# An attention and MoE kernel on one core: a gate one chunk later, down-scores in other PSUM banks, and a copy shared by two engines

## The chip, the core and the metric

The kernel runs on one core of one Trainium2 chip. A core has five engines with instruction streams of their own: TensorE (PE, matrix products into PSUM; PEld is its weight load), VectorE (DVE), ScalarE (ACT), GpSimd (POOL) and SyncE (SP, which here only issues transfers). Each works through its own list in order and waits at semaphores for the others. Transfers between the device's memory and on-chip SBUF run on 16 DMA engines that all queues share; SP's go through queue q1, POOL's through queue q0, and instructions are fetched through small queues of their own (q8, q14). The metric is the device time of one execution in microseconds (us). PSUM is the accumulator memory; the program uses three tiles of two banks (PA[0] to PA[2]) and two of one bank (PM[0], PM[1]).

## The reference

Two parts, one after the other:

```python
# q, k, v: (8 batches, 8 heads, 576 positions, 64)
q_d, k_d, v_d = mean over 4 neighbouring positions          # 144 positions
out_d     = softmax(q_d k_d^T / 8) v_d, each row repeated 4 times
out_local = softmax(q k^T / 8 where |i - j| < 4) v
x = (out_d + out_local) as (4608 tokens, 512)
h = x @ w_in                                                # 512 x 2048
y = (h * sigmoid(1.702 h)) @ w_out                          # 2048 x 512
```

Inputs and output are float32; the kernel multiplies in bf16.

## The kernel before, in words

**Tiling.** The 4608 tokens are nine groups of 512. For a group g, `mm1` makes h transposed in 16 blocks of 128 hidden columns (`hps_mm`, L616: four products of 128x512 each, one for each of the four chunks of 128 model columns), ACT applies SiLU into `gT`, and `mm2` makes four output tiles of 128 tokens with 16 products each (L672). A batch has 576 tokens, so the attention of batch g + 1 is woven into the products of group g: a dictionary of steps says ahead of which product a step of the attention is written. For group 0 the places are `POS_0 = [16, 18, 27, 54, 68, 60, 76]` and `VDP_0 = 52`, counted over 16 blocks of `mm1` and then the products of `mm2`; so 52 is ahead of the 37th product of `mm2`. The order of `mm2` in group 0 takes w_out in four parts of four hidden blocks, the third being wanted at its 33rd product.

**Attention of one batch.** Heads go in pairs (hp 0 to 3), pairs in two halves (qd 0 for pairs 0 and 1, qd 1 for pairs 2 and 3).
- q and k are loaded by POOL's queue (`load_qk`), transposed by DVE (`prep_1`, L260) and pooled over four positions by POOL (`pool_qk`, two additions for each of k and q). `pool_qk(b, qd, names)` can do k alone or q alone.
- `scores` makes the banded local scores (L351), `scores_d` the pooled ones (L369); ACT takes their exponentials (`exp_local`, `exp_down`) into es and eds.
- v is loaded by SP in ten transfers (`load_v`, L214), two for each of five chunks of positions, and cast to bf16 chunk by chunk (`prep_v`). For batches 0 and 1 the pooled v is made by products with a selection matrix (`prep_vd_pe`, L312) that ACT copies to vd (L321).
- `av_local` (L408) and `av_down` (L430) multiply with v; the row sums come along as a 65th column. `normalise` on DVE divides (L441, L443) into y.
- For batch 0, `turned` brings y to the transposed layout by products (`transp_sum`, L483, L493, L507) and `copy_x` writes xT (L520, L524): four copies for a pair, two for each of the two interleaved sets of positions (`par`).

**Order.** The schedule is manual: every engine carries out its instructions in the order in which the program writes them. Around the change, batch 0 is written out by hand ahead of the loop over groups. POOL pools the first half, then writes one element into w_in's buffer from v's buffer. That copy is the gate: it can't run before a certain v transfer has landed, and the load of w_in's first part (512 of 2048 columns) can't be issued before the gate. After it come the pooling of the second half, w_in's other two parts, the q and k loads of batch 1, two of four parts of w_out, and a memset.

On TensorE, `warm(n)` issues n products of zeros that write PM[0] and PM[1] in turn from one call to the next; the call ahead of `turned` writes PM[0]. Then batch 0's first products with h are placed between the four `turned` by `part`, which takes hidden blocks and model chunks: blocks 0 and 1 accumulate in the PM banks, 2 to 5 in halves of PA[1] and PA[2].

After that, the loop begins. On DVE it starts with the four transposes for batch 1 and then the gate of batch 1's v load, one element copied from w_out's first part:

```python
            load_v(1, gate=after(w_out_bf[0:1, 0, 0:1], nc.vector))
            pool_qk(1, 1)
            nc.gpsimd.tensor_copy(
                out=w_out_bf[0:1, 8, 0:1], in_=vf[1][0:1, 3, 0, 0:1]
            )
            load_w_out(2)
            load_w_out(3)
```

The last lines are one more gate of that kind: w_out's third and fourth part wait for v 1's fourth chunk.

Of the kernel before, what the change touches and what calls it, by code (L numbers as in the profile page):

```python
# [10 lines left out]
AF = mybir.ActivationFunctionType  # L11
# [8 lines left out]
def kernel(  # L20
# [9 lines left out]
    nc = tc.nc  # L30
    B, H, S, D = q.shape
    SD = S // 4
    HP = H // 2
# [5 lines left out]
    inv_sqrt_d = 1.0 / math.sqrt(D)  # L39
# [18 lines left out]
    w_in_bf = persist.tile([128, n_dmc, d_ff], BF16, name="w_in_bf")  # L58
# [5 lines left out]
    eds = [persist.tile([128, 2, 464], BF16, name=f"ed{i}") for i in range(2)]  # L64
# [3 lines left out]
    PA = [psum.tile([128, 2, 512], FP32, name=f"pa{i}") for i in range(3)]  # L68
    PM = [psum.tile([128, 512], FP32, name=f"pm{i}") for i in range(2)]
    turn = {"a": 0, "m": 0}  # L70

    def ps_tile(n=None):
        if n is None:
            n = turn["a"] % 3
            turn["a"] += 1
        return PA[n]

    def pm_tile():
        turn["m"] += 1
        return PM[turn["m"] % 2]  # L80
# [107 lines left out]
    qf, kf, vf = {}, {}, {}  # L188
# [46 lines left out]
    def load_w_in(c, n):  # L235
        nc.gpsimd.dma_start(
            out=w_in_bf[:, :, c : c + n],
            in_=bass.AP(
                tensor=moe_w_in.tensor, offset=moe_w_in.offset + c,
                ap=[[d_ff, 128], [128 * d_ff, n_dmc], [1, n]],  # L240
            ),
        )
# [23 lines left out]
    def prep_qk(b, qd):  # L266
        prep_1("k", b, qd)
        prep_1("q", b, qd)

    def pool_qk(b, qd, names="kq"):  # L270
        for name, src in (("k", kT), ("q", qT)):
            if name not in names:
                continue
            sv = src[b, qd].rearrange("p (j f) a -> p j f a", f=4)
            t1 = work.tile([128, SD, 2, 2], FP32, name="pq", tag="pq")
            nc.gpsimd.tensor_tensor(  # L276
                out=t1, in0=sv[:, :, 0:2, :], in1=sv[:, :, 2:4, :], op=ALU.add
            )
            if name == "k":
                dst = kdT[qd][:, 0:SD, :]  # L280
            else:
                t = work.tile([128, SD, 2], BF16, name=f"qdT{qd}", tag=f"qdT{qd}", bufs=1)
                qdT[b, qd] = t
                dst = t
            nc.gpsimd.tensor_tensor(
                out=dst, in0=t1[:, :, 0, :], in1=t1[:, :, 1, :], op=ALU.add
            )
# [73 lines left out]

    def scores_d(b, qd, sd=None):
        sd = sd or ps_tile()
        for kc in range(3):
            for a in range(2):
                for r in range(4):
                    rows = slice(32 * r, 32 * r + 32)
                    j = r % 2
                    nc.tensor.matmul(  # L369
                        sd[64 * j : 64 * j + 64, r // 2, SD * kc : SD * kc + SD],  # L370
                        lhsT=kdT[qd][rows, 48 * kc : 48 * kc + 64, a],
                        rhs=qdT[b, qd][rows, :, a],
                        start=(a == 0), stop=(a == 1),
                        tile_position=(32 * r, 64 * j),
                    )
        return sd
# [8 lines left out]
    def exp_down(qd, sd):  # L385
        nc.scalar.activation(  # L386
            out=eds[qd][:, :, 0:432], in_=sd[:, :, 0:432],
            func=AF.Exp, scale=inv_sqrt_d / 16.0,
        )
# [6 lines left out]
    def av(b, hp, n=None):  # L396
        o = ps_tile(n)
        av_local(b, hp, o)
        av_down(b, hp, o)
        return o  # L400

    def av_local(b, hp, o):
        E, vb = es[hp], vbs[b % 2]
        for i in range(5):
            for par in range(2):
                for j in range(2):
                    pos = j if par == 0 else 1 - j
                    nc.tensor.matmul(  # L408
                        o[64 * pos : 64 * pos + 64, par, 65 * i : 65 * i + 65],
                        lhsT=E[64 * par : 64 * par + 64, j, 60 * i : 60 * i + 64],  # L410
                        rhs=vb[64 * par : 64 * par + 64, i, 2 * hp + j, :],
                        start=True, stop=True,
                        tile_position=(64 * par, 64 * pos),
                    )

    def av_down(b, hp, o):
        Ed, vd, u = eds[hp // 2], vds[b % 2], hp % 2

        blocks = [(kc, x, 0) for kc in range(3) for x in range(2)]
        blocks += [(0, 0, 1), (0, 1, 1), (1, 0, 1), (2, 0, 1)]  # L420
        if True:
            for kc, x, c2 in blocks:
                for j in range(2):
                    pos = j if x == 0 else 1 - j
                    c0 = 65 * (5 + c2)
                    q0 = SD * kc + 48 * (min(x + c2, 1) + x)
                    last = x == c2 == 1
                    if last:
                        q0 = 0
                    nc.tensor.matmul(  # L430
                        o[64 * pos : 64 * pos + 64, j, c0 : c0 + 65],
                        lhsT=Ed[64 * j : 64 * j + 48, u, q0 : q0 + 64],
                        rhs=vd[64 * j : 64 * j + 48, kc, hp, :],
                        start=(kc == 0), stop=(kc == 2 or last),
                        tile_position=(64 * j, 64 * pos),
                    )

    def normalise(o):
        ov = o[:, :, 0:455].rearrange("p x (c e) -> p x c e", e=65)
        rc = work.tile([128, 2, 7, 1], FP32, name="rc", tag="rc")  # L440
        nc.vector.reciprocal(rc, ov[:, :, :, 64:65])  # L441
        y = work.tile([128, 2, 7, D], BF16, name="y", tag="y", bufs=4)
        nc.vector.tensor_tensor(  # L443
            out=y, in0=ov[:, :, :, 0:D],
            in1=rc.to_broadcast([128, 2, 7, D]), op=ALU.mult,
        )
        return y
# [69 lines left out]
    def copy_x(b, hp, x):  # L517
        t0 = b * S
        for par in range(2):
            nc.scalar.copy(  # L520
                out=sub(xT[hp], t0 + 3 + 57 * par, (114, 5), (1, 57)),
                in_=sub(x[par], 3 - 3 * par, (57, 5), (1, 57)),
            )
            nc.scalar.copy(  # L524
                out=sub(xT[hp], t0 + 573 * par, (1, 3)),
                in_=sub(x[par], 285 * par, (1, 3)),
            )
# [10 lines left out]
    def sub(t, off, *dims):  # L538
        return bass.AP(
            tensor=t.tensor, offset=t.offset + off,  # L540
            ap=[list(t.ap[0])] + [list(d) for d in dims],
        )
# [25 lines left out]
    def warm(n):  # L568
        if n:
            t = pm_tile()  # L570
            for _ in range(n):
                nc.tensor.matmul(
                    t, lhsT=wz[:, 0:128], rhs=wz, start=True, stop=True
                )

    def attention(b, slots=None):
        st = {}

        def s_pe(qd):
            st["s", qd] = scores(b, qd)  # L580
            st["d", qd] = scores_d(b, qd)
# [41 lines left out]
    def new_gT():  # L623
        return moe_sb.tile([128, n_ffc, TG], BF16, name="gT", tag="gT")
# [80 lines left out]
    o, y, x = {}, {}, {}  # L705
# [19 lines left out]
    sp = scores(0, 0, barred=True)  # L725
    exp_local(0, sp)
    prep_qk(0, 1)
    nc.gpsimd.tensor_copy(out=w_in_bf[0:1, 0, 0:1], in_=vf[0][0:1, 1, 0, 0:1])
    load_w_in(0, 512)
    pool_qk(0, 1)  # L730
    load_w_in(512, 512)
    load_w_in(1024, 1024)
    for qd in range(NQ):
# [6 lines left out]
    make_up()  # L740
    warm(5)
    sd = scores_d(0, 0)
    prep_v(0, nc.scalar, i=slice(0, 1))
    exp_down(0, sd)
# [5 lines left out]
        prep_v(0, nc.vector, i=slice(i, i + 1))  # L750
    warm(6)
    prep_vd_pe(0, PA[2])
    o[0] = PA[0]
    av_local(0, 0, o[0])
    av_down(0, 0, o[0])
    y[0] = normalise(o[0])
    sd = scores_d(0, 1, PA[1])
    exp_down(1, sd)
    nc.scalar.preload_act_table_set("silu_and_others")
    for hp in range(1, 3):  # L760
        o[hp] = PA[hp]
        av_local(0, hp, o[hp])
        av_down(0, hp, o[hp])
        y[hp] = normalise(o[hp])
    warm(1)

    gT0 = new_gT()
    acc = PM + [PA[n][:, u, :] for n in (1, 2, 0) for u in range(2)]
# [7 lines left out]
    def turned(hp, n):  # L776
        x = PM if n is None else [PA[n][:, u, :] for u in range(2)]
        transp_sum(y[hp], x)
        copy_x(0, hp, x)
# [20 lines left out]
    for g in range(n_groups):  # L800
        b = g + 1
        if g == 0:
# [6 lines left out]
                out=w_out_bf[0:1, 8, 0:1], in_=vf[1][0:1, 3, 0, 0:1]  # L809
# [61 lines left out]
```

The softmax here doesn't subtract the row's maximum and nothing guards it: scores larger than these inputs give would overflow.

## Time and profile before

| what | value |
|---|---|
| median of 8 executions | 333.97 us (332.78 to 336.96) |
| the profiled execution | 334.05 us |
| its span, first to last instruction | 332.3 us |
| TensorE busy | 316.2 us, 95% of the span |
| DVE, ACT, POOL busy | 130.9, 184.6, 138.4 us |
| dense products of `mm1` (L616), 544 in the group | 121.6 us busy |
| dense products of `mm2` (L672), 528 in the group | 121.7 us busy |
| moved by DMA | 41.36 MB, mean 124 GB/s |
| v load (L214) | 80 transfers of 128 KB, 5.4 us from issue to landing (median) |
| w_in | two parts of 512 KB, 6.3 us; one of 1024 KB, 9.8 us |

The profile is of one execution. Its own time (334.05 us) is the one that the span belongs to; what is over, 1.75 us, lies around the first and last instruction. A line of a timeline gives start, length, engine, line of the program, operation, output and inputs, how many instructions were merged, and in brackets the engine's idle time just before and what ended it. In the chain of waits, each line is a piece of the chain that ended last: start, length, what it was. TensorE's granted clock is given as a share of full speed (one digit for each fortieth of the span, in tenths).

### The profile page before, as it was taken

The page shows a single profiled execution, that of the slowest core. Times are in us where ns is not written, and L with a number is a line of the kernel's source. Part 1 is how long each engine was busy: PE and PEld are TensorE (multiplying, and loading weights), DVE is VectorE, ACT ScalarE, POOL GpSimd, SP SyncE. Part 2 cuts the span into 40 slices and gives each one's busy share as a digit, 9 for nine tenths or more (in the row PEclk, how much of TensorE's full clock was granted, in tenths as well). Part 3 has the DMA queues.
Part 4 walks back from the last instruction along what each step waited for, and adds up shares of the span by engine and source line. Part 5 has one row for each costly group of instructions (what it writes and reads, how often), then busy time and mean ns, then how long its engine had stood idle before and what let it go on. Part 6 is the DMA issues. An engine that isn't in the chain of part 4 may idle for free.

```text
span 332.3 us, 11272 instructions
## 1 busy us (share of the span) xinstructions
PE 316.2 (95%) x5043; PEld 159.4 (48%) x5043; DVE 130.9 (39%) x213; ACT 184.6 (56%) x323; POOL 138.4 (42%) x168
## 2 busy tenths in 40 slices
PE   8737999999999999999999999999999999999995
PEld 3425445444554445444544454455445554444444
DVE  4846402482167307730773077406740570000000
ACT  2524488257755665576656665666476746425611
POOL 7791834019900991099109910991089000000000
PEclk9967899999999999999999999999999999999999
DMA  7999969998931994199419940994180110011011
GB/s 123 172 184 211 176 136 190 194 184 212 189 94 54 215 190 119 46 210 194 128 40 215 208 114 36 198 212 109 59 175 3 36 65 32 2 64 63 2 59 67
DMA packets 63552, 41.36 MB, mean 124 GB/s; under 512 B 44048, under 2 KB 54416, under 8 KB 63504
## 3 DMA queue, kind: packets, MB, share of 16 engines
q1 hardware_dynamic: 55056, 26.95, 35.3%
q0 software_dynamic: 8304, 13.63, 23.4%
q8 instruction: 39, 0.64, 0.8%
q14 instruction: 9, 0.07, 0.1%
q10 hardware_dynamic: 144, 0.07, 0.1%
HBM read 44.83 MB, written 9.44 MB: 163 GB/s over the span
## 4 chain that ended last, share of the span: by engine, by line
PE 89%; SPq 4%; DVE 2%; DMA 2%; issue 1%; ACT 1%; DVEq 0%; ACTq 0%
PE pm L616 36%; PE pm L672 35%; SPq L214 4%; PE pa L351 3%; PE pa L616 2%; DMA vf<-in_v_dram 2%; PE pa L408 2%; PE pa L369 2%; PE pa L430 2%; PE pa L457 2%; PE pa L672 1%; PE pm L687 1%; DVE y L443 1%; PE pa L483 1%; ACT vd L321 0%
## 5 line engine op out<-in xcount | busy, mean ns | idle before, releaser
L616 PE MATMUL pm<-xT,w_in_bf 128*128 128x512 bf16 x544 | 121.6, 380 | 0.5 <-DVE xT L559 0.5
L672 PE MATMUL pm<-w_out_bf,gT 128*128 128x512 bf16 x528 | 121.7, 380 | 0.0
L627 ACT ACTIVATE gT<-pm 128x512 bf16<-128x512 f32 x136 | 81.1, 598 | 44.5 <-PE pm L616 44.5
L616 PEld LDWEIGHTS <-w_in_bf 128*128 128x128 bf16 x576 | 55.8, 98 | 67.9 <-issue 2.0
L672 PEld LDWEIGHTS <-gT 128*128 128x128 bf16 x560 | 51.8, 98 | 59.5 <-issue 0.2
L276 POOL TENSOR_TENSOR pq<-kT 128x576 f32<-128x576 bf16 x16 | 18.5, 1157 | 105.2 <-DVE kT L260 105.2
L394 DVE TENSOR_TENSOR es<-es,mask 128x600 bf16<-128x600 bf16 x28 | 20.1, 731 | 96.7 <-ACT es L380 95.9
L657 ACT ACTIVATE osb<-pm 128x512 f32<-128x512 f32 (+2 forms) x35 | 20.8, 593 | 39.3 <-PE pm L672 34.9
L532 ACT COPY od<-pa 128x384 f32<-128x384 f32 (+1 forms) x56 | 18.4, 412 | 30.8 <-DVE y L443 22.4
L443 DVE TENSOR_TENSOR y<-pa,rc 128x896 bf16<-128x896 f32 x32 | 34.9, 1092 | 1.1
L553 DVE TENSOR_TENSOR xT<-pa,od 128x570 bf16<-128x570 f32 x28 | 21.1, 754 | 10.4 <-ACT od L532 10.3
L380 ACT ACTIVATE es<-pa 128x600 bf16<-128x600 f32 x32 | 19.8, 669 | 6.6 <-PE pa L351 6.3
L297 POOL TENSOR_TENSOR v<-v 112x512 f32<-112x512 f32 x18 | 22.8, 1266 | 0.0
L659 DVE TENSOR_SCALAR osb<-pm 128x128 f32<-128x128 f32 x1 | 0.3, 292 | 55.3 <-ACT osb L657 55.3
L260 DVE STREAM_TRANSPOSE kT<-kb 128x576 f32<-128x576 f32 x16 | 20.0, 1250 | 3.1 <-DMA kb<-in_k_dram 3.0
L260 DVE STREAM_TRANSPOSE qT<-qb 128x576 f32<-128x576 f32 x16 | 19.9, 1241 | 0.9 <-DMA qb<-in_q_dram 0.8
L276 POOL TENSOR_TENSOR pq<-qT 128x576 f32<-128x576 bf16 x16 | 18.5, 1157 | 0.0
L291 POOL CAST vb<-vf 128x2560 bf16<-128x2560 f32 (+1 forms) x11 | 17.0, 1570 | 0.0
L441 DVE RECIPROCAL rc<-pa 128x14 f32<-128x14 f32 x32 | 7.7, 241 | 22.9 <-PE pa L430 22.9
L351 PEld LDWEIGHTS <-kT 32*64 32x64 bf16 x1280 | 11.9, 104 | 6.9 <-issue 5.9
L351 PE MATMUL pa<-qT,kT 32*64 32x60 bf16 x1280 | 13.8, 203 | 1.5 <-issue 1.1
L386 ACT ACTIVATE ed<-pa 128x864 bf16<-128x864 f32 x16 | 14.3, 896 | 1.5 <-PE pa L369 1.5
(86 smaller groups left out, 252.1 us busy)
## 6 DMA issues: line engine op xcount, KB each, us to landing
vf<-in_v_dram SPq DMA_DIRECT2D x80, 128.0 KB, 5.4
out_dram<-osb SPq DMA_DIRECT2D x35, 256.0 KB, 2.0
v<-in_v_dram SPq DMA_DIRECT2D x36, 192.0 KB, 5.2
kb<-in_k_dram POOLq DMA_DIRECT2D x16, 288.0 KB, 6.8
qb<-in_q_dram POOLq DMA_DIRECT2D x16, 288.0 KB, 7.7
w_out_bf<-in_moe_w_out_dram POOLq DMA_DIRECT2D x4, 512.0 KB, 12.7
w_in_bf<-in_moe_w_in_dram POOLq DMA_DIRECT2D x2, 512.0 KB, 6.3
w_in_bf<-in_moe_w_in_dram POOLq DMA_DIRECT2D x1, 1024.0 KB, 9.8
```

What stands on the lines that cost most here:

```text
L260: nc.vector.transpose(out=t32.rearrange("p (i c) -> p c i", c=18), in_=store[b, qd].bitcast(FP32).rearrange("p (c d) -> p c d", c=18),)
L276: nc.gpsimd.tensor_tensor(out=t1, in0=sv[:, :, 0:2, :], in1=sv[:, :, 2:4, :], op=ALU.add)
L297: eng.tensor_tensor(out=t1[0:112], in0=x[:, :, 0:2, :], in1=x[:, :, 2:4, :], op=ALU.add)
L351: nc.tensor.matmul(sp[r // 2][64 * par : 64 * par + 64, r % 2, 60 * i : 60 * i + 60], lhsT=kT[b, qd][rows, k0 : k0 + 64, a], rhs=qT[b, qd] ...
L380: nc.scalar.activation(out=es[2 * qd + u][:, :, 0:300], in_=sp[u][:, :, 0:300], func=AF.Exp, scale=inv_sqrt_d,)
L394: nc.vector.tensor_tensor(out=ev, in0=ev, in1=mask, op=ALU.mult)
L443: nc.vector.tensor_tensor(out=y, in0=ov[:, :, :, 0:D], in1=rc.to_broadcast([128, 2, 7, D]), op=ALU.mult,)
L553: eng.tensor_tensor(out=sub(xT[hp], t0 + 3, (57, 2), (114, 5), (1, 57)), in0=sub(x, 3, (509, 2), (57, 5), (1, 57)), in1=sub(od, 3, (57, 2) ...
L616: nc.tensor.matmul(acc, lhsT=w_in_bf[:, dmc, ffc * 128 : (ffc + 1) * 128], rhs=xT[dmc][:, g * TG : g * TG + TG], start=(dmc == 0), stop=(d ...
L627: nc.scalar.activation(out=gT[:, ffc, :], in_=acc, func=AF.Silu, scale=GELU_SCALE)
L657: eng.activation(out=osb, in_=ap, func=AF.Copy, scale=1.0 / GELU_SCALE)
L672: nc.tensor.matmul(ops[t], lhsT=gT[:, ffc, t * 128 : (t + 1) * 128], rhs=w_out_bf[:, ffc, :], start=(ffc == 0), stop=(ffc == n_ffc - 1),)
```

## The change

Three edits, all in the preparation of batch 0:

1. POOL pools k of the second half ahead of the gate of w_in, and q behind w_in's first load. The gate reads v 0's third chunk (index 2) instead of its second, so w_in's first load waits for the fifth v transfer where it waited for the third.
2. Batch 0's second down-scores go to PM[0] and PM[1], one bank for each pair of the half, instead of to PA[1]; their exponential is two ACT instructions of 432 columns instead of one of 864. TensorE's order is now: `av_local` of pairs 0 and 1, `av_down` of pairs 0 and 1, the down-scores, one warm product, then both products of pair 2. Before, it was pair 0, the down-scores, pair 1, pair 2, the warm product.
3. In `copy_x`, the two copies of the second set of positions (`par` 1) of the last pair are made by DVE instead of ACT.

```diff
     def scores_d(b, qd, sd=None):
         sd = sd or ps_tile()
+        bank = sd if sd is PM else [sd[:, u, :] for u in range(2)]
...
                     nc.tensor.matmul(
-                        sd[64 * j : 64 * j + 64, r // 2, SD * kc : SD * kc + SD],
+                        bank[r // 2][64 * j : 64 * j + 64, SD * kc : SD * kc + SD],
...
     def copy_x(b, hp, x):
         t0 = b * S
         for par in range(2):
-            nc.scalar.copy(
+            cp = nc.vector.tensor_copy if par and hp == HP - 1 else nc.scalar.copy
+            cp(
                 out=sub(xT[hp], t0 + 3 + 57 * par, (114, 5), (1, 57)),
                 in_=sub(x[par], 3 - 3 * par, (57, 5), (1, 57)),
             )
-            nc.scalar.copy(
+            cp(
                 out=sub(xT[hp], t0 + 573 * par, (1, 3)),
                 in_=sub(x[par], 285 * par, (1, 3)),
             )
...
     prep_qk(0, 1)
-    nc.gpsimd.tensor_copy(out=w_in_bf[0:1, 0, 0:1], in_=vf[0][0:1, 1, 0, 0:1])
+    pool_qk(0, 1, "k")
+    nc.gpsimd.tensor_copy(out=w_in_bf[0:1, 0, 0:1], in_=vf[0][0:1, 2, 0, 0:1])
     load_w_in(0, 512)
-    pool_qk(0, 1)
+    pool_qk(0, 1, "q")
     load_w_in(512, 512)
     load_w_in(1024, 1024)
...
     prep_vd_pe(0, PA[2])
-    o[0] = PA[0]
-    av_local(0, 0, o[0])
-    av_down(0, 0, o[0])
-    y[0] = normalise(o[0])
-    sd = scores_d(0, 1, PA[1])
-    exp_down(1, sd)
-    nc.scalar.preload_act_table_set("silu_and_others")
-    for hp in range(1, 3):
+    for hp in range(2):
         o[hp] = PA[hp]
         av_local(0, hp, o[hp])
+    for hp in range(2):
         av_down(0, hp, o[hp])
         y[hp] = normalise(o[hp])
+    scores_d(0, 1, PM)
+    for u in range(2):
+        nc.scalar.activation(
+            out=eds[1][:, u, 0:432], in_=PM[u][:, 0:432],
+            func=AF.Exp, scale=inv_sqrt_d / 16.0,
+        )
+    nc.scalar.preload_act_table_set("silu_and_others")
     warm(1)
+    o[2] = av(0, 2, 2)
+    y[2] = normalise(o[2])
```

## The prediction

> **What bounds the kernel now.** I read the page first (shares, clock row, chain), then the chain of waits in order of time, then the merged timeline from 0 to 74 us, and last the DMA records. The page says where nothing is to be had:
>
> ```profile
> PE 316.2 (95%) x5043; PEld 159.4 (48%) x5043; DVE 130.9 (39%) x213; ACT 184.6 (56%) x323; POOL 138.4 (42%) x168
> PEclk9967899999999999999999999999999999999999
> PE 89%; SPq 4%; DVE 2%; DMA 2%; issue 1%; ACT 1%; DVEq 0%; ACTq 0%
> ```
>
> TensorE is 95% busy, and the two dense lines (L616, L672) carry 70% of the chain. Only the first 40 us are bound by something else: slices 3 to 5 are where the clock is not full. All three edits lie there, so the question is how much sooner TensorE enters the dense stream, and whether that head start survives. The chain of waits, from the last v loads on (start, length, what):
>
> ```profile
> 13.25 0.64 SPq L214
> 13.94 7.31 DMA vf<-in_v_dram
> 22.29 0.81 ACT vd L321
> 23.14 0.54 PE pa L430 x19
> 23.68 0.89 PE pa L369 x19
> 24.60 0.90 ACT ed L386
> 30.20 1.49 issue
> ```
>
> Read it as a story. The tenth v transfer is issued at 13.94 and lands 7.31 us later, though the eight before it have landed by 15.5. Everything after hangs on it: the cast, the selection matmuls (L312), ACT's copy into vd, av_down, the second down-scores, their exp (TensorE stands still for 0.90 us, since the scores sit in PA[1], which av_local needs next), then a stall of 1.49 us that waits for nothing in the program. The timeline names the other clients:
>
> ```profile
> 13.04 0.80 POOL L236 DMA_DIRECT2D w_in_bf<-in_moe_w_in_dram  x1 [0.30 <-POOL w_in_bf L728]
> 13.86 1.16 POOL L276 TENSOR_TENSOR pq<-kT 128x576 f32<-128x576 bf16 x1
> 17.27 1.22 DVE L291 CAST vb<-vf 128x512 bf16<-128x512 f32 x2
> 21.35 0.43 DVE L291 CAST vb<-vf 128x512 bf16<-128x512 f32 x1 [2.85 <-DMA vf<-in_v_dram]
> 27.43 0.55 PE L483 MATMUL pm<-up,y 128*64 128x285 bf16 x4
> 31.61 1.26 DVE L260 STREAM_TRANSPOSE kT<-kb 128x576 f32<-128x576 f32 x1 [0.80 <-DMA kb<-in_k_dram]
> 37.98 0.14 DVE L708 CAST vf<-w_out_bf 1x1 f32<-1x1 bf16 x1 [1.22 <-DMA w_out_bf<-in_moe_w_out_dram]
> 46.81 0.18 POOL L808 CAST w_out_bf<-vf 1x1 bf16<-1x1 f32 x1 [6.34 <-DMA vf<-in_v_dram]
> 58.67 1.03 PE L672 MATMUL pm<-w_out_bf,gT 128*128 128x512 bf16 x4
> ```
>
> From the DMA records, per half us: where v runs alone (12 to 13 us) 377 and 378 of its 256 B records pass; from 16.0 to 18.5, beside w_in's first part, only 347 in five halves, with 387 records of 1024 B for w_in. From 18.5, w_in being through, 322 in one half. So w_in takes the last chunk's place, and DVE idles 2.85 us for it.
>
> **The change, part by part.**
>
> *1. w_in later.* POOL ends the batch-0 pooling at 11.10 and idles 1.46 us at the old gate. Now the k pooling of the second pair goes there (1.15 + 0.67, so 11.10 to 13.0). The new gate waits for the fifth v transfer, whose landing record is at 13.74: cast at 13.8, issue at 14.28 (the old spacing of 0.48), 1.24 us later than 13.04. The old issue needed 2.0 us to its first dozens of records and 2.5 to full pace (62 in the half from 15.5), so the new one gets up to pace about 16.8. The last two v transfers are issued at 13.25 and 13.94 as now; 2.3 us later they can flow (the first of their records come after 15.5), together 1024 records at 750 per us: the ninth is through at 16.3, most of the tenth by 16.8, its rest at the contended 140 per us by about 18. It cannot land later than now (21.25), nor does it help before DVE is free: vb's second and third chunk end at 18.49. So the fourth cast runs from 18.5 to 18.93 at best, against 21.78 now: between 0 and 2.85 us. I take 2.7, near the good end, because 370 of 512 records precede w_in. POOL may overlap less with DVE's selector work (2.03 us for two small operations beside POOL's pooling); if these shorten, up to 0.8 more.
>
> Behind the waiting POOL gate stand the q pooling (15.10 to 17.4 instead of 15.89 to 18.21), the two other w_in parts, the four qk loads of batch 1, two w_out parts and the memset. The k pooling has left that line, so all these issue about 0.8 us sooner, at 17.4 instead of 18.15. w_in's first part is wanted at 31.94 now (28.9 then) and landed at 20.29; its last landed at 28.78, first needed after 40. SP's queue is passed by nothing.
>
> *2. Down-scores to the MoE banks, two av_local ahead.* Now av_down to the first L483 takes 27.43 - 23.14 = 4.29 us. Then: av_local of pair 1 (0.49) goes under ACT's vd copy (0.80), which now covers only pair 0's 0.49, with 0.3 idle. Left: two av_down (0.54 each), scores (0.94), the exp of the first bank, the warm matmul (0.54), av of pair 2 (0.49 + 0.54, or 0.71 if it interleaves as the two pairs did, 1.42 for both). The stall is not gone: warm(1) writes PM[0], the very bank that the first exp reads, so it waits. That exp has 432 columns; from 0.598 for 512 and 0.896 for 864, 0.53, as an estimate. Sum 3.7 to 4.25 with 0.1 of gaps; I take 4.0, so 0.3 gained (0.05 to 0.6). The two exps cost ACT 1.06 instead of 0.89; with the table load (1.28) they end at 24.6, before the first copy_x at 25.6. y of pairs 0 and 1 (1.09 each) is done while TensorE makes scores.
>
> The next thing is the 1.49 us stall. Two stalls of TensorE's queue (1.08 ending at 14.35, 1.49 ending at 31.69) end 1.3 to 1.6 us after a 16 KB packet of the instruction queue (ended at 12.8 and 30.4). The block seems asked for some 5.7 us ahead, by the sequencer passing an instruction that the old program reaches right after the wait for exp at 25.54 and the new one after its wait at 22.8. So I move the stall along with the rest, gain 3.0, cost 0.
>
> By the Trainium skill (Runtime: NRT & Kernel Launch, Instruction fetch mechanics), crossing a 16 KiB boundary is mostly hidden; the 1.49 us here contradict that, and with no stall the sum would be 4.5 instead of 3.0.
>
> *3. Half of the last x copy on DVE.* ACT's four copies end at 37.96 and their reader (L616 with the last d_model chunk) starts at 39.18, behind ten matmuls of 0.216: ending 0.4 sooner gives 0. The price is the order on DVE: the copies (0.4 + 0.15, from half of the 0.754 of a 570-column sum) stand ahead of four transposes and the gate of v 1, which now run from 31.61, before TensorE has ended the transposition (37.08, then about 34.1). Transposes: 34.65 to 39.8 instead of 31.61 to 36.77. Scores of batch 1 (49.20, then 46.2) and POOL's pooling for them (39.8) leave 6 us: hidden. The v 1 gate moves from 37.98 to 39.8, and with it SP's ten v loads (38.26 to 40.1), their seventh landing (46.75 to 48.6), POOL's gate L808, w_out's third part (issue 49.1, landing 53.34 to 55.2) and v's casts. TensorE wants that part at 58.67 - 3.0 = 55.7. Slack falls from 5.3 to 0.5 us, so it stays hidden, barely; if that cover is gone it costs us for us. Casts end at 53.5, wanted at 56.6. This is what is late next.
>
> *Clock.* Granted is half from 19.4 to 29.6 and again from 33.05 to 36.46, in steps of 3.41. The step from 22.8 to 26.2 was 64% busy and did not lift; that from 29.6 to 33.05, 56% busy with the 1.49 stall in it, dropped. The same stall 3 us earlier falls into the step before and drops the next in the same way, so six dense matmuls run at 0.43 again: 0.
>
> The Trainium skill (TensorE: Matmul & The Clock Gate, Part 1) lets the clock fall only after an idle window of about 3.4 us; by that the new stall would cost no half-speed step and the sum would be 4.3 (six times 0.215 more). The 56% step speaks against it.
>
> Sum: 2.7 + 0.3 + 0 + 0 = 3.0. From 72 us on TensorE is dense at a period of 33.40 us per group (106.04, 139.44), so nothing gives it back. The profiled execution is 334.05 (span 332.3 and 1.75 around it), 0.08 above the median of the eight; 334.05 - 3.0 = 331.0.
>
> **The rivals.**
> *Chunk still late.* w_in reaches full pace before the tenth transfer flows, as now. For it: 140 records per us beside w_in mean 3.7 us for 512. Then it lands about 20.2 and 1.0 is gained, with part 2 1.3 at most: 332.7. Against: the 1.24 us. This is also "does not do what it says".
> *More is gained.* The instruction block comes in time, or the clock is up from 22.8 (that step's forerunner would be over 80% busy): 1.0 to 1.5 more, 329.6. Against: w_out's slack of 0.5 caps what is gained only ahead of the transposition on DVE's path.
> *Slower: w_out's third part becomes the bound.* Place: the 33rd matmul of L672. It decides against the change once that part lands 3 us after 55.7, that is v 1 coming 3.5 us slower than now. Nearest row: v 2, loaded beside q and k, took 12.1 us to its first landing against 2.9 for v 1; with 9.2 more the stall is 8.7 and the time 339.8. Against: w_out's second part ends about 39.9, so v 1 runs alone.
>
> **How the numbers follow.** About 0.5% (1.7 us) is what a measurement of this kernel can tell from no change. Forecast 0.58 (330.2 to 332.2), more gained 0.14, chunk late 0.18 (332.3 to 334), slower 0.10. So faster 0.72, same 0.18, slower 0.10. The range leaves out the slower case and the tips of the two others: 329.0 to 333.9.
>
> **What would show it.** In the new profile: w_in's first issue near 14.3; the fourth vb cast at 18.5 to 19 with almost no idle ahead; av_local of both pairs during the vd copy; a wait of warm on ACT of about 0.5; the first L483 near 24.4; an issue stall near 27 to 28.6; transposes from about 34.6; no wait at L672's 33rd matmul near 55.7; the first group's dense stream 3 us ahead and the same distance at the end. Wrong if the cast waits past 20, or if TensorE idles before w_out's third part.

## The result, and the profile after

The changed kernel takes 331.75 us (median of 19 executions, 327.41 to 333.43) against 333.98 us (56 executions, 331.16 to 336.96). The ratio is 0.9896, with a 95% interval of 0.9872 to 0.992: 3.5 us less (2.7 to 4.3). The ratio leaves out, as slow, executions over 1.5% above the fastest of the kernel (six of 20 of the changed one, the first profiled one among them); the medians of all differ by 2.2 us. Forecast were 3.0 us, which lies between the two, and a range of 329.0 to 333.9.

Two executions of the changed kernel were profiled, at 333.43 and 333.05 us. Both lie at the upper end of its spread (the second one's companions on the same chip took 329.03 to 331.18), so they are read for where time went, not for how much in all. First the timeline of the second one:

```profile
14.18 0.80 POOL L236 DMA_DIRECT2D w_in_bf<-in_moe_w_in_dram  x1 [0.30 <-POOL w_in_bf L731]
16.91 1.70 POOL L236 DMA_DIRECT2D w_in_bf<-in_moe_w_in_dram  x2
17.03 1.27 DVE L291 CAST vb<-vf 128x512 bf16<-128x512 f32 x3
23.14 0.55 PE L484 MATMUL pm<-up,y 128*64 128x285 bf16 x4
26.90 0.42 PE L508 MATMUL pa<-ident,y 60*64 60x57 bf16 x14 [0.70 <-issue]
34.47 1.25 DVE L260 STREAM_TRANSPOSE kT<-kb 128x576 f32<-128x576 f32 x1
38.80 0.16 DVE L710 CAST vf<-w_out_bf 1x1 f32<-1x1 bf16 x1
46.98 0.18 POOL L814 CAST w_out_bf<-vf 1x1 bf16<-1x1 f32 x1 [3.68 <-DMA vf<-in_v_dram]
```

w_in's load goes out at 14.18 instead of 13.04. DVE's three v casts now run without a gap (17.03 to 18.30); the 2.85 us of idle time ahead of the last of them is gone, and the last one ends 3.5 us sooner than at 21.78. The first turned product starts at 23.14 instead of 27.43. The transposes are late, as foreseen: 34.47 instead of 31.61. Now the chain of waits of the first profile (start, length, what), over the same places:

```profile
11.44 4.99 DMA vf<-in_v_dram
18.56 0.81 ACT vd L321
20.55 0.52 ACT ed L764
21.11 0.38 PE pm L574
21.95 0.30 PE pm L484 x4
23.82 3.72 issue
```

A v transfer is still on the chain, but it is the eighth, through at 16.4; the tenth landed at 17.07, 4.2 us sooner than before. The wait for the exp is there in its new form (0.52, the first bank only, in front of the warm product). And a stall of 3.72 us stands where 1.49 us stood. In this execution the first turned product was 5.55 us ahead and the product after the stall only 4.15 (31.69 to 27.54). The page of the same profile shows the other thing that is new, the clock, and the share of the stalls ("issue") on the chain:

```profile
PEclk9997999999999999999999999999999999999999
PE 89%; issue 3%; SPq 3%; DVE 2%; DMA 2%; ACT 1%; DVEq 0%; ACTq 0%
```

The clock drops for one slice instead of three (two, in the second profile). On the chain, issue grew from 1% to 3% (its pieces of 0.25 us and more add up to 2.75 us before, 8.4 us here, 5.2 us in the second profile).

The landmarks of all profiles, in us, from their timelines; "head start" is that of batch 1's scores over 49.20, the value before. The ratios are against the kernel before on the same chip.

| kernel | vd copy | first turned product | stall, its end | batch 1 scores | head start | ratio (95%) |
|---|---|---|---|---|---|---|
| before | 22.29 | 27.43 | 1.49, 31.69 | 49.20 | | |
| whole change | 18.56 | 21.88 | 3.72, 27.54 | 44.98 | 4.2 | 0.9896 (0.9872 to 0.992) |
| whole, again | 18.70 | 23.14 | 0.70, 26.90 | 45.60 | 3.6 | 0.9888 (0.9847 to 0.993) |
| edit 1 | 18.27 | 22.14 | 3.74, 27.82 | 46.33 | 2.9 | 0.9935 (0.9906 to 0.9964) |
| edit 2 | 22.39 | 26.86 | none | 46.35 | 2.8 | 0.9934 (0.9902 to 0.9967) |
| edit 3 | 20.34 | 25.48 | 1.75, 29.84 | 47.32 | 1.9 | 1.002 (0.9994 to 1.0047) |
| edits 1 and 2 | 19.05 | 22.37 | 1.89, 26.19 | 42.13 | 7.1 | 0.9888 (0.9843 to 0.9933) |
| edits 1 and 2, again | 18.36 | 21.68 | 2.82, 26.43 | 43.88 | 5.3 | 0.9883 (0.9838 to 0.9927) |
| edit 1, POOL's order alone | 20.69 | 25.83 | 1.60, 30.12 | 47.58 | 1.6 | 1.0045 (1.0009 to 1.0081) |
| edit 1, gate alone | 19.38 | 24.18 | 1.44, 28.69 | 47.14 | 2.1 | 0.9962 (0.9933 to 0.9992) |

One profile is one execution, and single executions differ by 2 us and more here: edit 3 alone shows a head start of 1.9 us with no gain in time, and the kernel before with nothing but 10 more rows (further down) has its scores at 46.95, 2.25 us ahead. So a head start in this table is worth no more than that spread, and the ratios decide.

### The profile page after: what moved, and what is told of

It reads as the page before. It is cut to its first block, busy times and chain, and to the rows that moved or that the text cites. A ratio compares the mean times of both kernels' runs of the same rounds, so it can differ in the third digit from the quotient of the medians.

```text
span 331.6 us, 11276 instructions
## 1 busy us (share of the span) xinstructions
PE 313.6 (95%) x5043; PEld 157.6 (48%) x5043; DVE 130.4 (39%) x215; ACT 184.2 (56%) x322; POOL 138.6 (42%) x168
## 4 chain that ended last, share of the span: by engine, by line
PE 89%; issue 3%; SPq 3%; DVE 2%; DMA 2%; ACT 1%; DVEq 0%; ACTq 0%
PE pm L618 36%; PE pm L674 35%; PE pa L351 3%; SPq L214 3%; PE pa L618 2%; PE pa L409 2%; PE pa L431 2%; PE pa L370 2%; PE pa L458 2%; PE pa L674 2%; DMA vf<-in_v_dram 2%; PE pm L689 1%; PE pa L484 1%; ACT vd L321 0%; PE pa L312 0%
## 5 line engine op out<-in xcount | busy, mean ns | idle before, releaser
L297 POOL TENSOR_TENSOR v<-v 112x512 f32<-112x512 f32 x18 | 22.8, 1265 | 0.0
L351 PE MATMUL pa<-qT,kT 32*64 32x60 bf16 x1280 | 14.2, 203 | 2.9 <-issue 1.8
L351 PEld LDWEIGHTS <-kT 32*64 32x64 bf16 x1280 | 12.1, 104 | 7.9 <-issue 6.8
L300 POOL TENSOR_TENSOR vd<-v 112x256 bf16<-112x256 f32 x18 | 13.7, 759 | 1.4
```

The source lines that it names most:

```text
L297: eng.tensor_tensor(out=t1[0:112], in0=x[:, :, 0:2, :], in1=x[:, :, 2:4, :], op=ALU.add)
L351: nc.tensor.matmul(sp[r // 2][64 * par : 64 * par + 64, r % 2, 60 * i : 60 * i + 60], lhsT=kT[b, qd][rows, k0 : k0 + 64, a], rhs=qT[b, qd] ...
```

## The experiments

Theory G says that the last chunk of v sets the start, and that its place behind w_in in the DMA queues is what edit 1 removes. Theory B gives the gain to edit 2. Theory F says that the blocks of TensorE's own instructions arrive too late, so that a head start is partly taken back.

**The whole change again.**

> The whole change once more, for a second profile. In the first profile of the changed kernel the first L484 (the first turned product) starts at 21.88 us where the kernel before had it at 27.43, so 5.55 us earlier, but a stall of TensorE's queue of 3.72 us (1.49 before) follows, and the time is only some 3.5 us shorter. Theory G (the last v chunk sets the start): the tenth v landing is again near 17, the fourth vb cast near 18, and the time 3 to 4 us below the kernel before. Theory F (an instruction block sets the resumption): whenever the first turned product starts, the stall in the middle of the second pair's turned products ends 5.5 to 6.5 us after the warm product that follows the exp. A theory that the first profile was a freak of the clock would show a stall of 1.5 us or less and a dense stream 5 us earlier.

Measured: ratio 0.9888. The tenth v landing is at 16.46, the casts end at 18.30, so G's numbers hold; F's window for the end of the stall, 5.5 to 6.5 us after the warm product, was met by the first profile (21.11 to 27.54) and missed by this one (21.88 to 26.90, 5.0 us). The stall's length is 3.72 in one and 0.70 in the other. The theory of a freak of the clock has its short stall, but not its dense stream 5 us earlier: the scores of batch 1 are 3.6 us ahead.

**Edit 1 alone.**

```diff
-    nc.gpsimd.tensor_copy(out=w_in_bf[0:1, 0, 0:1], in_=vf[0][0:1, 1, 0, 0:1])
+    pool_qk(0, 1, "k")
+    nc.gpsimd.tensor_copy(out=w_in_bf[0:1, 0, 0:1], in_=vf[0][0:1, 2, 0, 0:1])
     load_w_in(0, 512)
-    pool_qk(0, 1)
+    pool_qk(0, 1, "q")
```

> Only edit 1 (k pooling ahead of the gate, gate on the third chunk); down-scores, order and the x copy as before. Theory G: carries most of the gain: tenth v landing near 17 instead of 21.25, vb cast 4 near 18, time 2.5 to 3.2 us below before. Theory B (the order and the banks carry it): 0 to 1 us. Theory F: the old order reaches the block boundary after the exp of the full half, so the stall moves with it: ends 3 to 3.7 us earlier than 31.69.

Measured: 331.99 us, ratio 0.9935, that is 2.2 us less (1.2 to 3.1). The tenth landing is at 17.07. From its chain and timeline:

```profile
18.27 0.81 ACT vd L321
21.00 0.35 PE L408 MATMUL pa<-vb,es 64*64 64x65 bf16 x20 [0.99 <-ACT ed L386]
24.08 3.74 issue
```

The vd copy is 4.0 us ahead of before, the first turned product 5.3, the end of the stall 3.9 (F had 3 to 3.7). G has its landing; its gain of 2.5 to 3.2 lies partly in the interval. B's 0 to 1 us lies outside the interval. And F has its stall: it is 2.25 us longer, and of the 5.3 us ahead of it 3.9 are left behind it.

**Edit 2 alone** (the part of the diff from `prep_vd_pe` down, and `scores_d`).

> Only edit 2 (two av_local ahead, down-scores in the MoE banks, two exps, warm product ahead of pair 2); gate and x copy as before. Theory G: 0.05 to 0.6 us below before, as in the prediction's sum. Theory B: 1.5 to 3 us below. Theory F: the sequencer passes the boundary right after its first exp instead of after the whole exp, at most 0.5 us sooner, so the end of the stall moves by no more than 0.5 us whatever the work ahead of it gains.

Measured: 331.62 us, ratio 0.9934, 2.2 us less (1.1 to 3.3). So B is right on the size by itself, and the prediction's 0.3 us lies outside the interval. Yet the work ahead of the first turned product gained only 0.57 us, as the sum had it:

```profile
21.35 0.52 DVE L291 CAST vb<-vf 128x512 bf16<-128x512 f32 x1 [3.07 <-DMA vf<-in_v_dram]
25.59 0.59 PE L574 MATMUL pm<-wz 128*128 128x512 bf16 x1 [0.61 <-ACT ed L763]
26.86 0.55 PE L484 MATMUL pm<-up,y 128*64 128x285 bf16 x4
```

In this profile the stall of 1.49 us doesn't occur at all: the packet of TensorE's instructions comes at 27.51 where it came at 29.45, 1.9 us sooner for 0.57 us of work, and the place of the stall is passed near 29.9 instead of 31.69, where F allowed 0.5 us. With the stall went the second spell of half clock: half speed from 20.86 to 31.10 here, from 19.40 to 29.64 and once more from 33.05 to 36.46 before. That is where the head start grows from 0.57 to 2.85 us. Whether the stall stays away in every execution of edit 2, a single profile can't say, and a head start of 2.25 us occurs without edit 2 too. So the gain is measured, and what makes it up beyond the 0.57 us is read from one profile and not shown.

**Edit 3 alone.**

```diff
+            cp = nc.vector.tensor_copy if par and hp == HP - 1 else nc.scalar.copy
-            nc.scalar.copy(
+            cp(
```

> Only edit 3 (half of the last x copy on DVE). All theories: same time within 0.5 us; the four transposes start near 37.7 instead of 31.61, since they stand behind the copy on DVE, and the gate of v 1 at about 43 instead of 37.98, w_out's third part lands about 58 to 58.5, against 58.67 at its first reader: the slack of 5.3 us is nearly gone. The rival that this is a loss by itself: 1 to 3 us slower with TensorE idle ahead of the 33rd product of L672.

Measured: 334.96 us, ratio 1.002 (0.9994 to 1.0047): between 0.2 us gained and 1.6 us lost. Transposes from 36.19, the gate of v 1 at 40.52, w_out's third part landed at 55.26 and its first reader ran at 57.2: 2 us of slack, where the kernel before had 5.3 and next to none was expected (transposes near 37.7, landing at 58). No idle time ahead of the 33rd product.

The three ratios multiply to 0.9889: within intervals of some 0.3% each, the edits add up to the whole.

**Edits 1 and 2 without edit 3**, run twice.

> Edits 1 and 2 without edit 3: all four copies of the last pair stay on ACT, so DVE's transposes of batch 1 start as soon as q and k are there. Theory C (edit 3 costs what comes behind it on DVE): 0.5 to 1.2 us faster than the whole change, that is 4 to 4.7 us below before; the transposes start near 30.3, the gate of v 1 near 36.5 to 37 instead of 38.2, and from the scores of batch 1 to those of batch 2 it takes about 34.1 us, without the queue stall of 0.8 to 1.5 us that the whole change has at 65 to 67. Rival (edit 3 is free, as the prediction has it): same time as the whole change within 0.3 us, and the stretch stays at 35 us.

> Edits 1 and 2 without edit 3 once more, since the first time had few undisturbed executions. The single edits measured so far (ratios 0.9935, 0.9934 and 1.002) multiply to 0.9889, the whole change's own. Theory C (edit 3 costs 0.7 us): 0.987 of before. Rival (free): 0.989. In its first profile the stretch between the scores of batch 1 and 2 was 35.0 us here too, with 0.65 us of waiting ahead of the 33rd product of L674; if that is the limit, the third part of w_out lands within 0.5 us of that product again.

Measured: 0.9888 and 0.9883 (330.59 and 331.29 us), against 0.9896 and 0.9888 for the whole change. The difference is under the measurement, so edit 3 is told neither from free nor from a loss of some tenths; this version doesn't beat the changed kernel by more than can be told. C's mechanism falls: the stretch from the scores of batch 1 to those of batch 2 is 35.0 and 35.4 us here too, where C wanted 34.1. The first of these profiles, the fastest of all profiled executions (span 326.9 us), shows something else:

```profile
36.66 0.14 DVE L710 CAST vf<-w_out_bf 1x1 f32<-1x1 bf16 x1 [1.22 <-DMA w_out_bf<-in_moe_w_out_dram]
52.45 1.04 PE L674 MATMUL pm<-w_out_bf,gT 128*128 128x512 bf16 x4 [0.64 <-DMA w_out_bf<-in_moe_w_out_dram]
```

With a head start of 7.1 us TensorE arrives at the 33rd product before w_out's third part has landed (52.40) and waits 0.64 us. This is the place of the rival that was to make the kernel slower; in this profile it takes back what is gained beyond some 6 us. In the second one that part landed at 52.21, 1.1 us ahead of its reader (53.34), so there it was not the limit.

**Edit 1 split: POOL's order without the gate, the gate without the order.**

```diff
+    pool_qk(0, 1, "k")
     nc.gpsimd.tensor_copy(out=w_in_bf[0:1, 0, 0:1], in_=vf[0][0:1, 1, 0, 0:1])
     load_w_in(0, 512)
-    pool_qk(0, 1)
+    pool_qk(0, 1, "q")
```

> Of edit 1 only the order on POOL: k pooling ahead of the gate, but the gate still on the second chunk (landed near 12.5); the rest as before. k pooling ends at 13.0, so w_in's first load is issued at about 13.5 instead of 13.04. If the wait for the third chunk is what keeps the last v chunk free of w_in (theory G): 0.2 to 0.8 us below before, v's tenth landing still near 20 to 21. If the pooling ahead does most of it (0.5 us of delay and DVE rid of POOL beside it): landing at 17.5 to 18.5 and 1.5 to 2 us below before.

```diff
-    nc.gpsimd.tensor_copy(out=w_in_bf[0:1, 0, 0:1], in_=vf[0][0:1, 1, 0, 0:1])
+    nc.gpsimd.tensor_copy(out=w_in_bf[0:1, 0, 0:1], in_=vf[0][0:1, 2, 0, 0:1])
```

> Of edit 1 only the gate: it reads the third chunk, and POOL's order stays (gate, load, then k and q pooling together). The gate opens near 13.6, so w_in's first load is issued near 14.1 as in the whole change; k pooling starts after it, at 14.9, and q pooling ends near 18.8, w_in's other parts 2 us later than in edit 1. Theory G (the time of the gate is the gain): the tenth v landing is near 17, the fourth vb cast near 18 to 18.5, time 1.5 to 2.5 us below the kernel before, as with all of edit 1. If the pooling order is needed too: the later q pooling holds up the second down-scores (wanted at 19.9) or the DVE casts beside it, and the time is within 1 us of the kernel before.

Measured: the order alone 334.42 us, 1.0045 (1.0009 to 1.0081), slower by 1.5 us (0.3 to 2.7) by the ratio, but the medians differ by only 0.4 us (334.42 against 334.06), so that it gains nothing is shown, and a loss hardly. The gate alone 333.51 us, 0.9962 (0.9933 to 0.9992), 1.3 us less (0.3 to 2.2), between G's 1.5 to 2.5 and its rival's 1. Their last casts (order alone, then gate alone):

```profile
13.27 0.80 POOL L236 DMA_DIRECT2D w_in_bf<-in_moe_w_in_dram  x1 [0.30 <-POOL w_in_bf L729]
19.86 0.43 DVE L291 CAST vb<-vf 128x512 bf16<-128x512 f32 x1 [1.96 <-DMA vf<-in_v_dram]
```

```profile
14.41 0.80 POOL L236 DMA_DIRECT2D w_in_bf<-in_moe_w_in_dram  x1 [0.30 <-POOL w_in_bf L728]
16.48 2.51 DVE L291 CAST vb<-vf 128x512 bf16<-128x512 f32 x3
```

So the time at which w_in is issued decides over the last chunk. Issued at 13.5 or sooner (six profiles: before, edits 2 and 3, the order alone, and the two further down that add rows to the kernel before) the tenth landing comes between 19.20 and 21.65; issued from 13.9 on (eight profiles) between 16.46 and 17.28. The gate alone keeps the whole q and k pooling behind the load: q pooling ends at 19.5 and w_in's other parts go out at 19.45 instead of 17. Its three casts take 2.51 us instead of 1.27, beside POOL's pooling. So the order gains nothing without the gate. Whether it adds to the gate the ratios don't settle: 1.3 us alone and 2.2 us with the order, in intervals that overlap.

**Where the stall stands.** The listing of TensorE's instructions has its stall of 1.49 us at row 960 and that of 1.08 us at row 448 or just below; these are 512 rows apart. If blocks of 256 rows lie behind it, added rows must move the stalls by as many rows. The rows were added without more work, by cutting warm products into narrower pieces:

```diff
-    warm(19)
+    warm(19, 128)        # 76 products of 128 columns instead of 19 of 512
...
-    warm(5)
+    warm(5, 128)
```

> The whole change, with the first and second block of warm products cut into pieces of 128 columns (76 and 20 instead of 19 and 5; the same columns in total): 144 more instruction rows on TensorE ahead of everything, nothing else. Theory F (instruction blocks of 256 rows are asked for when the one before is entered, and take 5 to 6.5 us while the queues are full): the block is entered during av_local (about 18 to 18.5 us) instead of after the exp (21.1); the long stall moves 144 rows forward, into the first pair's turned products, and ends at 24 to 25 instead of 27.5; time 0.8 to 1.6 us below the whole change. Theory G or a cause in the data: the stall stays inside the second pair's turned products at the same place of the program, and the time is the same.

> The whole change with 220 more rows ahead (first block of warm products in pieces of 128 columns, second in pieces of 64, third in pieces of 128). Theory F: a block border falls just behind the selection products and the next one into the products between the second and third pair's turned products; two stalls instead of one, the first ending near 23.8, the second at 28.5 to 29.5, so the batch 1 scores come 0 to 1.5 us later than in the whole change; time the same to 1.5 us longer. Theory G: same time, same place of the stall.

The second one has `warm(19, 128)`, `warm(5, 64)` and `warm(6, 128)`. The long stalls in the two chains, first with 144 rows, then with 220:

```profile
12.59 2.08 issue
19.43 0.88 issue
23.58 2.66 issue
```

```profile
11.43 3.50 issue
20.13 1.27 issue
25.03 2.56 issue
32.60 1.19 issue
```

By the borders at rows 448, 704, 960 and 1216, less 144, the stalls must stand at 304, 560 and 816: in the listing these are the second scores (L351), av_local (L409) and the end of the first pair's turned products (L508), and there they stand. Less 220, at 228, 484, 740 and 996: the first down-scores (L370), the selection products (L312), av_down of pair 2 (L431) and the third pair's first turned product (L484); all four agree. The places are F's, and a cause in the data is out. The times are not what F said: 331.77 us (0.9928, 0.9896 to 0.9959) with 144 rows, no gain over the whole change, as the stall ended at 26.24 and not at 24 to 25, and others came at 12.59, 19.43 and 63.65; and 335.67 us (1.0036, 1.0 to 1.0072) with 220 rows, 4 to 5 us above the whole change where 0 to 1.5 were foreseen.

**How far ahead a block is asked for.**

```diff
-    warm(5)
+    warm(5, 256)         # 10 more rows, in the kernel before
```

```diff
-    warm(6)
+    warm(6, 128)         # 36 more rows, in the kernel before
```

> The kernel before, with its second block of warm products in pieces of 256 columns: 10 more rows ahead. Theory L (the queue runs about 64 rows ahead of a waiting product, so a block border is passed before or after a wait according to whether it stands within 64 rows of it): the border that the kernel before has about 86 rows behind its wait for the exp is now 76 behind it, still out of reach. So nothing changes: the instruction packet comes 3.5 to 4.5 us after the end of that wait, the stall in the second pair's turned products stays at 1 to 2 us, the time within 1 us of before. If rows as such matter: the same change as with 36 rows.

> The kernel before, with its third block of warm products in pieces of 128 columns: 36 more rows ahead, so the border is 50 rows behind the wait for the exp. Theory L: the sequencer passes it while the wait is still on, and the packet comes 2.2 to 3.2 us after the end of the wait instead of 3.5 to 4.5; the stall moves to the first of the second pair's turned products and shrinks by about 0.5 us; time 0.3 to 1.2 us below before. Without the look-ahead: packet 3.5 to 4.5 us after the wait, the stall grows by the 0.7 us by which the border is reached sooner, time the same.

Measured: 334.02 us (0.9986, 0.9951 to 1.002) and 335.75 us (1.0021, 0.9992 to 1.0049). The packet of the instruction queue came 3.6 us after the end of the wait for the exp with 10 rows (23.67 to 27.23) and 4.2 us with 36 rows (26.07 to 30.29). Theory L wanted 2.2 to 3.2 in the second case, so it falls. The stall with 36 rows, ahead of the second pair's first turned product, shows in the timeline:

```profile
26.07 0.49 PE L408 MATMUL pa<-vb,es 64*64 64x65 bf16 x20 [0.99 <-ACT ed L386]
32.49 0.55 PE L483 MATMUL pa<-up,y 128*64 128x285 bf16 x4 [2.57 <-issue]
```

It stands 36 rows ahead of the old place and is 1.1 us longer, since the program reaches the border sooner and the block comes no sooner.

## Why the prediction was right, and where not

The sign, the range and nearly the size were right: 3.0 us forecast, 3.5 measured by the ratio and 2.2 by the medians. The terms behind the sum were less good, and that it came out so near is in part luck: edit 2 gave far more than its 0.3 us, and stalls further on, which the prediction put at nothing, took much of the head start back.

*Edit 1, 2.7 us.* It measured 2.2 (1.2 to 3.1) by itself. The mechanism was as described: the tenth landing came at 16.5 to 17.1, not 18, and DVE was free sooner (casts from 17.03 with its selector work out of the way, 0.58 instead of 2.03 us for the two selector operations). Against the one profile of the kernel before, the vd copy gained 3.6 to 4.0 us. But that profile has one of the later landings: in the six with the old gate the copy starts between 20.34 and 22.82, at 21.5 on the average, in the six with the new gate and no added rows at 18.7. That is 2.8 us, and the 2.7 was right.

*"So I move the stall along with the rest, gain 3.0, cost 0".* This step failed in edit 1's profile and the first one of the whole change: there the stall grew from 1.49 to 3.7 us. From the end of the wait for the exp to the resumption it takes 6.4 us (whole change), 6.8 (edit 1) and 5.0 (whole change, second profile), 6.15 before: only in the second profile did the block's delay shrink, by 1.1 us. In the first two of these profiles the clock stayed full up to 28.1 and 26.9, the products in between ran faster, and more of the delay showed as stall; in the third, at half clock from 19.6, 0.70 us of it did. By these profiles, moving everything along is right only at an unchanged clock.

*Edit 2, 0.3 us.* This is the mis-sized term: 2.2 (1.1 to 3.3). The 0.57 us up to the first turned product are inside the prediction's 0.05 to 0.6 (its terms add up to 3.8 to 4.2, not 3.7 to 4.25; the stretch took 3.6 us here). What was left out is what follows: in that profile the instruction packet came 1.9 us sooner and there was no stall. That this is the whole of the difference is not shown.

*Clock, 0.* The prediction held the half-speed steps to move along. Time at half speed, worked out from each execution's mean clock, fell from 14.1 us (74 executions before) to 6.4 us (20 of the whole change); it is 9.4 with edit 1 and 11.2 with edit 2. Among the executions before, one us more at half speed goes with 0.23 us more time, which would make 1.8 us of the 7.7. That is an association and not an experiment: stalls and clock come together.

The weighing of the clock rule stands: the Trainium skill (TensorE: Matmul & The Clock Gate, Part 1) lets the clock fall after an idle window of about 3.4 us. In the first profile of the whole change it fell at 28.1, after a step of 3.41 us (from 24.70) in which TensorE was idle for 2.84 us and had resumed at 27.54. With edit 1 alone it fell at 26.86, 2.78 us into the stall. In the steps before these falls TensorE was busy for 17% and 18%, so no step was wholly idle, and the rows are stricter than the rule. (The step from 22.8 to 26.2, put at 64% busy in the prediction, is 61% in the trace; nothing hangs on it.)

The other one, that crossing a block border is mostly hidden (Runtime: NRT & Kernel Launch, Instruction fetch mechanics), is contradicted by 0.7 to 3.7 us of stall in nine of the ten profiles of the table. The same section's 256 instructions for a block of 16 KiB agree with the places of the stalls.

*Edit 3, 0.* Consistent: 1.002 alone, no difference without it. The working was close: transposes from 33.85 and 34.47 against 34.65, though the gate of v 1 opened at 38.80 and not 39.8, because the four transposes followed each other at 1.08 us and not 1.29.

*The slower rival, w_out's third part.* In the whole change the slack at the 33rd product was 1.6 us in the first profile (landed 52.97, read at 54.53) and 2.2 in the second, where 0.5 was forecast. The rival's place was right: in the fastest profile of edits 1 and 2 it had 0.64 us.

*"So nothing gives it back."* This step failed too. The first profile's 4.2 us of head start at batch 1's scores ended as 0.7 us of span (332.3 to 331.6), the second's 3.6 as 1.1. In both, further stalls of TensorE's queue stand on the chain later on, at 65.6, 126.1 and 227.4 us in the first (1.47, 0.81, 1.04 us), where the profile before has none over 0.3 us from 63.3 us on:

```profile
65.59 1.47 issue
126.10 0.81 issue
227.44 1.04 issue
```

These three amount to 3.3 us, and 3.5 were lost. By the ratio 3.5 us are kept over the executions; why these later stalls come in some executions and not in others was not tried and stays open.

## What to carry to other kernels

When a late transfer bounds a stage, look at what shares its queues at that moment: holding a big load back by 1.1 us brought the last part of the small one in 3.5 us sooner (means of eight and six profiles). Moving only the work around the gate gained nothing. A head start is worth only what the next late thing leaves of it, so follow it through to the first place where an instruction block or a later load is waited for. And before explaining a microsecond by one profile, take a second one: here they differed by 3 us in one stall.

## What the runs showed that was not expected

- TensorE's instruction stream is itself a transfer that can be late. Its borders lie 256 rows apart in the listing; adding 144 and 220 rows moved the stalls by just that, and 220 rows cost 4 to 5 us with the same columns to multiply. One such row is a weight load or a product, however short.
- A packet of 16 KB for these instructions came 1.9 to 4.5 us after the wait that the request stood behind (twelve profiles), and where TensorE had stalled it went on 1.2 to 1.6 us after the packet's end.
- DVE's small operations took 0.58 us for the two selector steps when POOL was not computing beside them, and 1.66 to 2.05 us when it was; the cost of POOL's work on DVE moves to the DVE operation beside it (in the second profile, the 245-column step took 1.96 us instead of 0.76; with edit 1 alone it was over before POOL began, and took 0.41).
- POOL's new order without the new gate gains nothing: 1.5 us slower by the ratio (0.3 to 2.7), 0.4 by the medians. Why was not looked for.
